# Chunk 0 of a gated network multiplied before its 1/rms is known, behind strided attention, on one core

## Chip, cores and metric

The kernel runs on one core of a Trainium2 chip. The metric is the device time of one execution in microseconds (us); several executions give a median.

## What is computed

Attention with two fixed masks on 8 batches of 8 heads, then RMS norm and a gated feed-forward network over all 4608 rows, in fp32:

```
scores = q @ k.T / sqrt(64)                # 8 x 8 heads, 576 x 576, head_dim 64
rel = pos[:, None] - pos[None, :]
mask_local   = (rel >= 0) & (rel < 32)                        # heads 0 to 3
mask_strided = (rel >= 0) & (pos[None, :] % 32 == pos[:, None] % 32)   # heads 4 to 7
attn = softmax(where(mask, scores, -1e9)) @ v
x = attn as (4608, 512)                    # batch * seq, head * head_dim
xn = x / sqrt(mean(x * x, -1) + 1e-6) * rms_g
out = (silu(xn @ w_gate) * (xn @ w_val)) @ w_out              # 512 -> 1536 -> 512
```

The weights arrive as float64.

## The kernel before

**Layout.** The 4608 rows are nine chunks of 512. x is held with the 512 model features on the partitions, as four tiles (kc = 0 to 3) per chunk. The network's 1536 inner features are twelve groups of 128, u = 0 to 11: for each u the gate product and the value product (`gemm1`, banks g and v) each take 12 multiplications of 128x512 (4 tiles times 3), then `slot_g` and `slot_h` form silu(gate) * value, and `slot_o` multiplies that with w_out into the banks a0 to a3. Each fp32 operand is split into a high and a low part (`split`), and a product is high*high + low*high + high*low, hence the 3. Chunks 0 to 2 run in this way, with weights that are read from float64 and split in chunk 0 (`convert_weights`: two ScalarE operations, then sign, merge, cast and low part); chunks 3 to 8 run two at a time with a scheme of seven products.

**Attention.** A unit is a pair of heads of one batch: `unit_s` multiplies the scores (72 small multiplications, and for units 0 to 3 two more that put the mask, `cb`, into the bank through the identity `identb`), takes maxima, exps, sums and scaled weights, and transposes on VectorE; `unit_o` multiplies with the values (80 small multiplications) and copies the result into x. Chunk 0 needs units 0 to 3. Unit 0 uses the bank pair, units 1 to 3 use a0/a1, a2/a3 and g/v; all units alternate between two buffers for exps (`pp`), two for the transpose (`pT`) and two for maxima and sums (`st`).

**Chunk 0's norm.** `square` squares each tile; its column sums go into a corner of a1 (`sums`, L663). `root0` then adds them up, takes a bit trick as a first guess of 1/sqrt and three Newton steps (L712 to L719, VectorE), spreads the result over the partitions (`spread`, L724, TensorE) and multiplies the four tiles by it and by the gain (L729). Only then `convert(0)` splits x and the first `gemm1` can start.

**Order.** Everything is issued in an order that a planner in the program (`Plan`) makes from a table of costs: it gives each operation an engine and a place in that engine's row, and the engines run their rows in order. Where TensorE would stand for long in the beginning the planner puts filling multiplications by zeros (`fill`, L470) into the row. Loads go through SyncE's queue, a few at the start through ScalarE's.

## Time and profile before

| | us |
|---|---|
| median of 3 executions | 988.3 (987.5 to 989.18) |
| the profiled execution | 984.86 |
| its span | 982.7 |

| engine | busy us | share of the span | instructions |
|---|---|---|---|
| TensorE, multiplications (PE) | 946.3 | 96% | 8621 |
| TensorE, weight loads (PEld) | 769.2 | 78% | 8621 |
| VectorE (DVE) | 726.4 | 74% | 1125 |
| ScalarE (ACT) | 450.2 | 46% | 713 |
| GpSimd (POOL) | 159.5 | 16% | 122 |

The span is what the profiler sees of the program; the execution's own time holds a little more. The chain of work that ended last is 89% TensorE and 5% VectorE. Busy shares are means over stages, so the stretches below are read one by one.

### The profile page before, as it was taken

Reading aid. Unit: us, or ns where it says so; the run is one execution under the profiler, and the core shown is the slowest. Engines: PE = TensorE matmul, PEld = TensorE weight load, DVE = VectorE, ACT = ScalarE, POOL = GpSimd, SP = SyncE. Lnnn points to the kernel's source line nnn. Section 1 sums busy time; section 2 is a strip of 40 time slices with the busy share of each in tenths; the row PEclk is TensorE's granted clock in tenths of the full one; section 3 lists DMA queues with packets and bytes.
Section 4 is the critical chain, followed back from the end, with each engine's and each line's share of the span. In section 5 each row is a group of like instructions: output and inputs, shape, how many; then the busy total and the mean of one; then the engine's idle time right before and its main releaser. Section 6 shows DMA issues by size and latency. Waiting matters only on the chain.

```text
span 982.7 us, 21097 instructions
## 1 busy us (share of the span) xinstructions
PE 946.3 (96%) x8621; PEld 769.2 (78%) x8621; DVE 726.4 (74%) x1125; ACT 450.2 (46%) x713; POOL 159.5 (16%) x122
## 2 busy tenths in 40 slices
PE   6999999999989999899999999999999999999998
PEld 5878887888768888688888777788787887888786
DVE  4599889789778997866668999545778894344783
ACT  5697665333245321644445574244444733333340
POOL 1211002023036330200003403001112020000130
PEclk8799999999989999899999999999999999999999
DMA  9746656878655848784643936974246579833631
GB/s 366 284 153 192 229 198 227 292 243 302 202 191 201 275 149 274 279 258 127 190 148 114 318 105 239 385 255 121 57 122 212 171 260 385 265 107 95 216 97 65
DMA packets 122495, 205.66 MB, mean 209 GB/s; under 512 B 10784, under 2 KB 66336, under 8 KB 119328
## 3 DMA queue, kind: packets, MB, share of 16 engines
q1 hardware_dynamic: 121680, 203.58, 62.2%
q8 instruction: 68, 1.11, 0.4%
q10 hardware_dynamic: 720, 0.74, 0.2%
q14 instruction: 27, 0.22, 0.1%
HBM read 160.24 MB, written 44.04 MB: 208 GB/s over the span
## 4 chain that ended last, share of the span: by engine, by line
PE 89%; DVE 5%; DMA 2%; ACT 2%; issue 2%; SPq 0%; ACTq 0%; DVEq 0%
PE a L1006 15%; PE g L1006 10%; PE v L1006 10%; PE v L863 9%; PE g L863 9%; PE a L900 9%; PE a L1129 8%; PE g L1129 5%; PE v L1129 4%; PE pair L605 4%; PE pair L547 3%; DVE bl L454 2%; DMA bl<-gvd 1%; PE v L470 1%; DMA to<-bl 1%
## 5 line engine op out<-in xcount | busy, mean ns | idle before, releaser
L446 ACT CAST bl<-bl 128x512 fp32r<-128x512 f32 (+1 forms) x170 | 109.6, 668 | 120.0 <-PE a L900 28.9
L1006 PE MATMUL a<-bl,bl 128*128 128x512 f32 x644 | 159.7, 393 | 0.0
L454 DVE TENSOR_TENSOR bl<-bl,bl 128x512 fp32r<-128x512 f32 x201 | 149.6, 773 | 11.8 <-ACT bl L446 3.8
L1006 PEld LDWEIGHTS a<-bl,bl 128*128 128x128 f32 x644 | 119.2, 188 | 26.1 <-ACT bl L1013 0.4
L863 PE MATMUL g<-bl,bl 128*128 128x512 f32 x432 | 114.7, 400 | 6.9 <-DVE bl L454 6.2
L1006 PE MATMUL g<-bl,bl 128*128 128x512 f32 x425 | 110.4, 394 | 6.9 <-DMA bl<-gvd 3.4
L1006 PE MATMUL v<-bl,bl 128*128 128x512 f32 x420 | 109.2, 395 | 3.8 <-DVE bl L1043 3.2
L863 PE MATMUL v<-bl,bl 128*128 128x512 f32 x432 | 112.6, 396 | 0.0
L900 PE MATMUL a<-bl,bl 128*128 128x512 f32 x432 | 109.0, 393 | 0.0
L863 PEld LDWEIGHTS g<-bl,bl 128*128 128x128 f32 x432 | 80.3, 190 | 27.0 <-DVE bl L454 8.5
L1006 PEld LDWEIGHTS g<-bl,bl 128*128 128x128 f32 x425 | 80.2, 190 | 25.6 <-DVE bl L454 5.9
L1006 PEld LDWEIGHTS v<-bl,bl 128*128 128x128 f32 x420 | 79.4, 190 | 22.5 <-DVE bl L1043 4.4
L1017 DVE TENSOR_TENSOR a<-a,bl 128x512 f32<-128x512 f32 x72 | 49.9, 697 | 63.7 <-PE a L1006 51.4
L900 PEld LDWEIGHTS a<-bl,bl 128*128 128x128 f32 x432 | 82.0, 190 | 17.9 <-DVE bl L454 0.7
L863 PEld LDWEIGHTS v<-bl,bl 128*128 128x128 f32 x432 | 80.8, 190 | 17.8 <-DVE bl L883 0.4
L963 DVE TENSOR_TENSOR bl<-bl,bl 128x512 f32<-128x512 f32 x98 | 69.4, 723 | 30.1 <-ACT bl L1022 29.7
L1129 PE MATMUL a<-bl,bl 128*128 128x512 f32 x298 | 70.3, 390 | 0.0
L454 POOL TENSOR_TENSOR bl<-bl,bl 128x512 fp32r<-128x512 f32 x23 | 33.8, 1471 | 213.6 <-PE a L1006 101.6
L448 DVE CAST bl<-bl 128x512 fp32r<-128x512 f32 (+1 forms) x90 | 48.2, 537 | 27.3 <-PE a L900 7.2
L1129 PEld LDWEIGHTS a<-bl,bl 128*128 128x128 f32 x298 | 55.9, 188 | 11.7
L963 POOL TENSOR_TENSOR bl<-bl,bl 128x512 f32<-128x512 f32 x21 | 38.8, 1847 | 116.7 <-DVE bl L963 46.5
L815 POOL TENSOR_TENSOR bl<-bl 128x256 f32<-128x256 f32 (+1 forms) x32 | 32.7, 1030 | 135.7 <-DVE bl L808 59.8
(150 smaller groups left out, 1299.6 us busy)
## 6 DMA issues: line engine op xcount, KB each, us to landing
bl<-gvd SPq DMA_DIRECT2D x252, 256.0 KB, 4.9
gvd<-bl SPq DMA_DIRECT2D x72, 256.0 KB, 4.2
bl<-to SPq DMA_DIRECT2D x72, 256.0 KB, 4.8
bl<-wos SPq DMA_DIRECT2D x54, 256.0 KB, 3.8
bl<-in_wgv_dram SPq DMA_DIRECT2D x12, 1024.0 KB, 8.6
bl<-wos SPq DMA_DIRECT2D x12, 1024.0 KB, 6.6
vt<-in_vl_dram SPq DMA_DIRECT2D x28, 320.0 KB, 3.5
xx<-in_kT_dram SPq DMA_DIRECT2D x28, 288.0 KB, 4.4
```

What stands on the lines that cost most here:

```text
L446: nc.scalar.copy(out=o, in_=i)
L448: nc.vector.tensor_copy(out=o, in_=i)
L454: elementwise(CH, lambda e: both(e).tensor_tensor(out=lo.new(F32R), in0=src(), in1=hi.f32(), op=ALU.subtract), reads + [hi.key], [lo.key])
L547: nc.tensor.matmul(out=pr[at // CH][c:c + 32, at % CH:at % CH + KW], lhsT=tq()[r, q0:q0 + 32], rhs=tk_()[r, q0:q0 + KW], start=not quick, ...
L605: nc.tensor.matmul(out=pr[s][64 * h:64 * h + 64, 32 * lo:32 * hi], lhsT=va()[r:r + 32, kb], rhs=pT[r:r + 32, 64 * kb - 32 * (kb > 0):min(6 ...
L815: elementwise(256 if ds != ALL else CH, lambda e: both(e).tensor_tensor(out=d.t[:, ds], in0=x.t[:, xs], in1=y.t[:, ys], op=ALU.subtract), ...
L863: nc.tensor.matmul(out=out_, lhsT=w.t[:, sl], rhs=x.t, start=(kc == 0 and i == 0), stop=(kc == KC - 1 and i == 2))
L900: nc.tensor.matmul(out=acc[t], lhsT=x.t[:, sl], rhs=w.t, start=(u == 0 and i == 0), stop=(u == NU - 1 and i == 2))
L963: elementwise(CH, lambda e: both(e).tensor_tensor(out=o.new() if fresh else o.t, in0=a.t, in1=b.t, op=how), [a.key, b.key], [o.key])
L1006: nc.tensor.matmul(out=banks[bk], lhsT=w, rhs=xs[k][y].t, start=start and k == 0 and i == 0, stop=stop and k == 1 and i == 2, skip_group_c ...
L1017: op("DVE", dve(CH), 0, lambda: nc.vector.tensor_tensor(out=banks[bk], in0=banks[bk], in1=t.t, op=ALU.add), reads=[t.key], writes=[bk])
L1129: nc.tensor.matmul(out=banks[bks[j]], lhsT=v, rhs=xs[k][y].t, start=start and k == 0 and i == 0, stop=stop and k == KT - 1 and i == 2, ski ...
```

## The change

1. **Chunk 0 is multiplied without its norm.** `convert0` splits each tile as soon as its unit is there, with the gain folded in; 1/rms per row is applied later: as a factor to the gate product ahead of silu (a product on VectorE with a spread copy of 1/rms), and, as the value product also lacks it, as a factor per output row where the output banks are copied out.
2. **`root0`** keeps the first four operations on VectorE; the Newton steps, now four operations each, go to GpSimd; the spread copy of 1/rms is taken by ScalarE.
3. **Units 0 to 3** use the banks g/v, a0/a1, a2/a3 and pair; units 2 and 3 get exp and transpose buffers of their own out of the pool of blocks, and four `st` tiles replace two. The u = 1 products of chunk 0 use a0 and a2, and that pass calls `slot_h` ahead of `slot_o`.
4. **Loads** come in a written order (`LOADS`): q/k of unit 0, identity and gain, mask, q/k of units 1 and 2, and so on; the first weights stand ahead of the last two values.
5. **Sign of weights:** the VectorE operation that took a sign bit out of one 32-bit word and put it into another becomes a 16-bit mask from one half-word to another; ScalarE writes the exponent's bits into the neighbouring half-word.
6. Fillings are 192 columns wide instead of 224, are counted anew, and go to the bank of the operation that follows. The choice of blocks uses `MIX` = 30 instead of 40.

```diff
-MIX = 40
+MIX = 30
-FILLS = 150.0
+FILLS = 120.0
+FILLN = 192
+LOADS = ("q0", "c2", "c0", "q1", "q2", "v0", "c1", "q3", "v1", "w", "v2", "v3")
...
     def banks_of(i):
-        k = i if i < NPRO else 0
-        if k == 0:
+        if i >= NPRO or i == NPRO - 1:
             return [pair_[:, 0], pair_[:, 1]], [SK]
-        two = (("a0", "a1"), ("a2", "a3"), ("g", "v"))[k - 1]
+        two = (("g", "v"), ("a0", "a1"), ("a2", "a3"))[i]
...
+        if 1 < i < NPRO:
+            z, y = take2(), take2()
+            pbuf_, pkeys, tbuf_, tkeys = (lambda: wide(z, None, SW)), keys_of(z), (lambda: wide(y, None, SW)), keys_of(y)
...
-            for k in range(3):
-                nc.vector.tensor_tensor(out=rz, in0=rx, in1=ry, op=ALU.mult)
-                V(out=rz, in0=rz, scalar=-0.5, in1=ry, op0=ALU.mult, op1=ALU.mult)
-                V(out=rcol if k == 2 else ry, in0=rz, scalar=1.5, in1=ry, op0=ALU.add, op1=ALU.mult)
-        op("DVE", 3200, 0, root, reads=["a1s%d" % p for p in range(4)], writes=["rcol"])
+        op("DVE", 760, 0, first, reads=["a1s%d" % p for p in range(4)], writes=["rx"])
+        def newton():
+            T = nc.gpsimd.tensor_tensor
+            for k in range(3):
+                T(out=rz, in0=ry, in1=ry, op=ALU.mult)
+                T(out=rz, in0=rz, in1=rx, op=ALU.mult)
+                nc.gpsimd.tensor_scalar(out=rz, in0=rz, scalar1=-0.5, scalar2=1.5, op0=ALU.mult, op1=ALU.add)
+                T(out=rcol if k == 2 else ry, in0=rz, in1=ry, op=ALU.mult)
+        op("Pool", 2400, 0, newton, reads=["rx"], writes=["rcol"])
...
-        for kc in range(KC):
-            rt = raw[0, kc]
-            op("DVE", dve(CH) + 60, 0, lambda kc=kc, rt=rt: nc.vector.scalar_tensor_tensor(
-                out=rt.t, in0=rt.t, scalar=gt[:, kc:kc + 1], in1=acc[3], op0=ALU.mult, op1=ALU.mult),
-               reads=["a3", "gt"], writes=[rt.key])
+        r = E["root"] = take()
+        op("ACT", act(CH, True), 0, lambda: nc.scalar.copy(out=r.new(), in_=acc[3]), reads=["a3"], writes=[r.key])
...
+    def convert0(kc):
+        rt, hi, lo, k = raw[0, kc], take(True), take(True), gt[:, kc:kc + 1]
+        op("ACT", act(CH), 0, lambda: nc.scalar.activation(out=hi.new(F32R), in_=rt.t, func=AF.Copy, scale=k), reads=["gt", rt.key], writes=[hi.key])
+        op("DVE", dve(CH), 0, lambda: nc.vector.scalar_tensor_tensor(out=lo.new(F32R), in0=rt.t, scalar=k, in1=hi.f32(), op0=ALU.mult, op1=ALU.subtract),
+           reads=["gt", rt.key, hi.key], writes=[lo.key], port=True)
+        X[kc] = hi, lo
+        give(rt)
...
-        op("DVE", dve(2 * CH), 0, lambda: nc.vector.scalar_tensor_tensor(out=cell(0), in0=cell(1), scalar=0x80000000, in1=cell(0),
-                                                                         op0=ALU.bitwise_and, op1=ALU.bitwise_or), writes=wk + [("wq", 2)], port=True)
+        op("DVE", SIGN, 0, lambda: nc.vector.tensor_scalar(out=half(1), in0=half(3), scalar1=0x8000, scalar2=None, op0=ALU.bitwise_and),
+           writes=wk + [("wq", 2)], port=True)
...
-        return key[0]
+        return {"g": "a0", "v": "a2"}[key[0]] if c == 0 and key[1] == 1 else key[0]
...
+        if c == 0:
+            r = E["root"]
+            op("DVE", dve(CH), 0, lambda: nc.vector.tensor_tensor(out=e.new(), in0=bg, in1=r.t, op=ALU.mult), reads=[bk, r.key], writes=[e.key])
+            op("ACT", act(CH), 0, lambda: nc.scalar.activation(out=e.t, in_=e.t, func=AF.Silu), writes=[e.key], tab="silu")
...
-                    copy_to(e, ob.new(), acc[t])
+                    if c:
+                        copy_to(e, ob.new(), acc[t])
+                    elif e == "ACT":
+                        nc.scalar.activation(out=ob.new(), in_=acc[t], func=AF.Copy, scale=rcol[:, t:t + 1])
+                    else:
+                        nc.vector.tensor_scalar(out=ob.new(), in0=acc[t], scalar1=rcol[:, t:t + 1], scalar2=None, op0=ALU.mult)
```

**Where the rows of the engines change.** ScalarE, from the exps of the first unit on, before. `pair`, `a_`, `g` and `v` are banks, `pp` the exp buffers, `st` maxima and sums; L565 is an exp, L446 a copy of unit 0's result into x, L772 the first operation on the first weights (`bl_217`):

```order
L565 ACTIVATE pp_69,st_76<-pair,st_76 128x64 x9
L565 ACTIVATE pp_70,st_77<-a_83,st_77 128x64 x5
L565 ACTIVATE pp_70,st_77<-a_84,st_77 128x64 x4
L565 ACTIVATE pp_69,st_76<-a_85,st_76 128x64 x5
L565 ACTIVATE pp_69,st_76<-a_86,st_76 128x64 x4
L446 COPY bl_452<-pair 128x288
L565 ACTIVATE pp_70,st_77<-g,st_77 128x64 x5
L565 ACTIVATE pp_70,st_77<-v,st_77 128x64 x4
L772 ACTIVATE bl_217<-bl_217 128x1024
```

The same place now, from the third unit's exps on (L582 is an exp, L452 a copy into x, L765 a high part of x with the gain, L808 and L812 the operations on weights):

```order
L582 ACTIVATE bl_386,st_78<-a_87,st_78 128x64 x5
L582 ACTIVATE bl_386,st_78<-a_88,st_78 128x64 x4
L582 ACTIVATE bl_461,st_79<-pair,st_79 128x64 x9
L452 COPY bl_520<-a_85 128x288
L452 COPY bl_520<-a_86 128x224
L452 COPY bl_524<-a_86 128x64
L765 ACTIVATE bl_530<-bl_514,few 128x512
L765 ACTIVATE bl_586<-bl_520,few 128x512
L808 ACTIVATE bl_217<-bl_217 128x1024
```

The four runs of exps follow one another, and copies, splitting and weights come behind them.

TensorE at the end of the prologue, now. L689 are sums of squares, L564 scores of a unit of the next chunk, L476 fillings, L901 gate and value products of u = 0 (`bl_530` and `bl_602` are high and low part of the first x tile), L754 spreads 1/rms:

```order
L564 MATMUL pair<-xx_64,xx_63 32x64 x36
L689 MATMUL a_86<-few,bl_657 128x4 x4
...
L476 MATMUL a_85<-still 128x192
L901 MATMUL g<-bl_530,bl_718 128x512 x2
L901 MATMUL g<-bl_602,bl_718 128x512
L901 MATMUL v<-bl_530,bl_718 128x512 x2
L901 MATMUL v<-bl_602,bl_718 128x512
L901 MATMUL g<-bl_586,bl_718 128x512 x2
L901 MATMUL g<-bl_646,bl_718 128x512
L901 MATMUL v<-bl_586,bl_718 128x512 x2
L901 MATMUL v<-bl_646,bl_718 128x512
L754 MATMUL a_88<-ident,few 128x128 x4
```

Before, the spreading (L724) stood between 29 and 32 fillings ahead of the first product; it now stands behind the first 12 products, and 21 fillings stand ahead of them.

VectorE at the same place, now. L814, L816, L454 and L819 are sign, merge, cast and low part of weights (`bl_217` the first set, `bl_266` the second), L766 the low part of the last x tile, L737 to L740 the start of 1/rms:

```order
L814 TENSOR_SCALAR bl_217<-bl_217 128x1024
L816 SCALAR_TENSOR_TENSOR bl_217<-bl_217 128x1024
L766 SCALAR_TENSOR_TENSOR bl_661<-bl_657,few,bl_661 128x512
L454 CAST bl_718<-bl_217 128x1024
L737 TENSOR_REDUCE few<-a_86 128x4
L738 TENSOR_SCALAR few<-few 128x4
L739 TENSOR_SCALAR few<-few 128x4
L740 TENSOR_SCALAR few<-few 128x4
L819 TENSOR_TENSOR bl_718<-bl_217,bl_718 128x1024
L588 SCALAR_TENSOR_TENSOR pp_69<-pair,cb 128x576
L591 TENSOR_REDUCE st_76<-pp_69 128x9
L814 TENSOR_SCALAR bl_266<-bl_266 128x1024
```

Before, nine Newton operations (L717 to L719) and four scalings of x (L729) stood behind L715 here; both are gone from VectorE's row, and the second weight set is not begun until the low part of the first is done.

## Rows read from the trace of the kernel before

**Rows 1.** Busy time by stretch: from and to in us, length, then per engine busy us (and instructions), granted TensorE clock as a share of 2.4 GHz, busy share of the DMA engines, GB/s.

```profile
0.00:51.00 51.00, 40.79 (x858) 35.55 (x859) 26.62 (x65) 30.26 (x96) 9.29 (x18) 0.80 0.82 314
51.00:160.00 109.00, 108.06 (x1033) 87.99 (x1033) 101.50 (x125) 77.73 (x96) 11.84 (x9) 1.00 0.59 202
160.00:983.00 823.00, 797.49 (x6733) 645.68 (x6731) 598.32 (x937) 342.24 (x522) 138.40 (x97) 0.99 0.62 204
```

**Rows 2.** TensorE's waits from 60 us on, the five longest kinds: who waited for whom, us in total, times, the longest.

```profile
PE g L863 <- DVE bl L454: 5.6, 3, 2.9
PE g L1006 <- DMA bl<-gvd: 3.4, 1, 3.4
PE v L1006 <- DVE bl L1043: 3.2, 3, 1.6
PE pair L691 <- DVE bl L448: 2.4, 2, 1.8
PE g L1006 <- DVE bl L454: 1.7, 1, 1.7
```

**Rows 3.** TensorE in order of time: start, length, line, operation, out<-in, shape, count, and in brackets the idle time before it and what ended it.

```profile
7.12 0.41 PE L541 MATMUL pair<-cb,identb 128*128 128x320 bf16 x2 [0.99 <-DMA cb<-in_consts_dram]
7.46 1.21 PE L547 MATMUL pair<-bl 64*32 64x64 f32 x72
...
42.34 4.65 PE L470 MATMUL v<-still 128*128 128x224 bf16 x29
...
47.74 3.23 PE L470 MATMUL v<-still 128*128 128x224 bf16 x32
50.74 0.71 PE L863 MATMUL g<-bl,bl 128*128 128x512 f32 x2
52.04 0.50 PE L863 MATMUL g<-bl,bl 128*128 128x512 f32 x1 [0.58 <-DVE bl L454]
```

**Rows 4.** ScalarE in order of time, columns as in rows 3.

```profile
5.44 0.30 ACT L500 CAST ident<-identb 128x128 f32<-128x128 bf16 x1 [1.80 <-DMA identb<-in_consts_dram]
9.80 0.31 ACT L565 ACTIVATE pp<-pair,st 128x64 f32<-128x64 f32 x1 [4.07 <-PE a L547]
...
16.04 0.31 ACT L565 ACTIVATE pp<-a,st 128x64 f32<-128x64 f32 x1 [0.80 <-DVE st L586]
...
21.45 0.40 ACT L446 COPY bl<-pair 128x288 f32<-128x288 f32 x1 [2.63 <-PE pair L605]
...
24.36 1.17 ACT L772 ACTIVATE bl<-bl 128x1024 f32<-128x1024 f32 x1
...
36.63 0.68 ACT L446 COPY bl<-g 128x256 f32<-128x256 f32 x2 [6.88 <-PE v L605]
37.10 0.74 ACT L446 COPY bl<-v 128x256 f32<-128x256 f32 x2
37.81 0.63 ACT L659 ACTIVATE bl<-bl 128x512 f32<-128x512 f32 x1
```

**Rows 5.** VectorE in order of time, columns as in rows 3.

```profile
42.52 0.18 DVE L712 TENSOR_REDUCE a<-a 128x4 f32<-128x16 f32 x1 [3.44 <-PE a L663]
...
44.96 0.16 DVE L719 SCALAR_TENSOR_TENSOR few<-a,few 128x4 f32<-128x4 f32 x1
...
48.01 1.41 DVE L729 SCALAR_TENSOR_TENSOR bl<-bl,few,a 128x512 f32<-128x512 f32 x2 [0.21 <-issue]
```

**Rows 6.** TensorE where it restarts after idle time that no semaphore ended ("issue"), columns as in rows 3; between the first row and the second stand seven more, with 4, 1, 1, 40, 32, 5 and 9 multiplications.

```profile
13.83 0.75 PE L547 MATMUL a<-bl 64*32 64x64 f32 x35 [2.16 <-issue]
...
20.11 1.27 PE L605 MATMUL pair<-pT,bl 32*64 32x64 f32 x71 [1.28 <-issue]
...
26.71 2.33 PE L605 MATMUL a<-pT,bl 32*64 32x64 f32 x80
...
33.03 1.28 PE L663 MATMUL a<-few,bl 128*128 128x4 f32 x11 [1.24 <-issue]
```

**Rows 7.** The DMA queue that carries instructions, in the microseconds 17 to 18 and 30 to 31: packets, MB, time as a share of 16 engines.

```profile
q8 instruction: 1, 0.02, 6.0%
...
q8 instruction: 1, 0.02, 5.5%
```

**Rows 8.** The issue of the first half of the mask through ScalarE's queue, from the DMA issues of the first 20 us: out<-in, count, KB each, us from issue to landing.

```profile
cb<-in_consts_dram ACTq DMA_DIRECT2D x1, 144.0 KB, 5.4
```

**Rows 9.** GpSimd's operations by line and shape over the whole span: count, busy us, mean ns of one, idle time before.

```profile
L815 POOL TENSOR_TENSOR bl<-bl 128x256 f32<-128x256 f32 x26 | 24.0, 933 | 93.5 <-PE v L863 55.5 <-DVE bl L815 19.5 <-DVE bl L808 17.8
...
L808 POOL TENSOR_TENSOR bl<-bl 128x1024 f32<-128x1024 f32 x5 | 12.7, 2538 | 11.0 <-DVE bl L750 9.0 <-DVE bl L700 2.0
...
L463 POOL MEMSET few<- 128x7 f32 x1 | 0.1, 105 | 0.0
```

**Rows 10.** VectorE's operations by line and shape from 0 to 165 us, columns as in rows 9.

```profile
L776 DVE SCALAR_TENSOR_TENSOR bl<-bl 128x1024 uint32<-128x1024 uint32 x18 | 21.9, 1216 | 0.7 <-ACT bl L774 0.4 <-issue 0.3
...
L883 DVE TENSOR_TENSOR bl<-bl,v 128x512 f32<-128x512 f32 x12 | 8.2, 684 | 3.8 <-PE v L863 3.7
...
L448 DVE CAST bl<-bl 128x1024 fp32r<-128x1024 f32 x6 | 4.1, 690 | 0.1
```

**Rows 11.** Busy time by stretch as in rows 1, around the fillings of rows 3.

```profile
42.00:46.00 4.00, 4.00 (x24) 3.32 (x24) 2.75 (x14) 4.00 (x5) 0.00 (x0) 0.51 0.86 269
48.00:50.00 2.00, 2.00 (x23) 2.00 (x22) 1.99 (x4) 0.56 (x2) 0.00 (x0) 1.00 0.08 25
```

More of the change, by code (lines that the diff above doesn't have):

```diff
@@ L347, in op @@
                 g = gen[home[k[1]]]
-                if g.first:
-                    continue
-                if g.fresh is True:
+                if g.fresh is True and not g.first:
                     g.fresh = fn
@@ L1219, in pair_of_chunks, with due @@
             give(dst)
-    def done(i):
-        if i == 3:
-            root0()
-            convert(0)
-    for i in range(NPRO):
-        load(i)
-        load_v(i)
+    def due(z):
+        return z[1] if z[0] == "gv" else 2 * z[1] + OLAG
+    queue = sorted([("gv", u) for u in range(NU)] + [("o", k) for k in range(KT)], key=due)
+    for z in LOADS:
+        if z[0] == "q":
+            load(int(z[1]))
+        elif z[0] == "v":
+            load_v(int(z[1]))
+        elif z[0] == "c":
+            load_consts(int(z[1]))
+        else:
+            plan.boost = WB
+            convert_weights(*queue.pop(0))
+            plan.boost = 0.0
     plan.boost = BP
@@ L1246, in prepare @@
             convert_weights(*queue.pop(0))
-    queue = sorted([("gv", u) for u in range(NU)] + [("o", k) for k in range(KT)], key=due)
     prepare(AHEAD)
```

129 lines of the change are left out of this document (79 added, 50 removed).

## The prediction

> **What bounds the kernel now.** I read the busy time by stage first, then TensorE's waits, then the rows of each engine up to the first product. The profiled execution splits into three stretches [rows 1]. Up to 51 us no product of the gated network runs, although TensorE shows 40.8 us busy: that is scores, values and filling multiplications. From 51 to 160 us TensorE is busy 108.06 of 109 us, with VectorE close behind it at 101.5 and ScalarE at 77.7. Afterwards TensorE is busy 797.5 of 823 us, and its five longest kinds of wait behind 60 us sum to 16.3 us [rows 2]. So after the first 51 us only TensorE's own work counts, and what can move the end is (1) when chunk 0's first product starts, (2) whether VectorE still feeds it, (3) those later waits.
>
> The end of the first stretch [rows 3]: 29 fillings from 42.34, the spreading multiplication, 32 fillings from 47.74, two products at 50.74 and then a wait for VectorE (the first low part of x) until 52.04. Taking those two at 0.23 us each off 52.04, the products run without a hole as if begun at **51.6**.
>
> What holds them until then is one chain: scores, exps, values, squares, their sums (TensorE, until about 42.5), VectorE's root from 42.52 to 45.1, spreading, four scalings from 48.01, splitting [rows 3, 4, 5]. In ScalarE's rows the first run of exps starts at 9.80, the third at 16.04 after 0.80 us of waiting for VectorE's use of a shared buffer, and the fourth stands behind a copy, at 21.45, that waits 2.63 us for the values of unit 0; they end at 24.36, where the first weights begin [rows 4].
>
> One more thing holds TensorE. At 13.83, 20.11 and 33.03 it restarts in the middle of a run of equal multiplications, after 2.16, 1.28 and 1.24 us in which it waited for nothing that the profile names [rows 6]. From the first restart to the second it issues 127 multiplications (35+4+1+1+40+32+5+9), from the second to the third 254, that is twice 127. In the microsecond from 17 and in that from 30, shortly ahead of two of the restarts, the instruction queue moves one packet of 0.02 MB [rows 7]. I read it as the next block of the program arriving late: between two restarts lie 6.3 us, and the block behind a boundary seems to be asked for when the boundary before it is crossed. 222 multiplications stand ahead of 13.83 (30 fillings, 74 of unit 0, 74 of unit 1, 5 fillings, 39 of unit 2), so boundaries lie at 95, 222, 349, 476, 603, 730. 95 is the 63rd of unit 0's 72 score multiplications, which begin at 7.46 and take 1.2: near 8.45, and 222 could be passed 5.4 us later; 349 6.3 us after that; 603 5.0 us after 476, the 45th of the 80 values of unit 1 that begin at 26.71: near 28.0 [rows 3, 6]. All of it with the DMA engines 0.82 busy over the stretch [rows 1].
>
> [...]
>
> **The change, step by step.**
> *First scores.* The mask was third on ScalarE's queue, landed 5.4 us after issue and held the first score to 7.12; identb, which lay behind one 288 KB load as the mask now does on SyncE's queue, let ScalarE go on at 5.44 [rows 3, 4, 8]. With 30 narrower fillings (224 to 192 columns) ending near 5.7, I take 5.9: **1.2 us earlier**.
>
> *Exps.* A run takes 2.6 us (the fourth: 21.75 to 24.36). Unit 2's scores still hit boundary 222 (104 multiplications to the end of unit 0, 178 after unit 1, 4 fillings), now at 12.6; their other half takes 0.75, the maximum about 1.1. So the runs start at 8.7, 11.4, 14.5, 17.1 and end at 19.8 instead of 24.36: own banks and buffers take away both waits.
>
> *Values.* Unit 0's follow 20 fillings; 349 is the 19th of those: 12.6+6 = 18.5. Boundary 476 falls on multiplication 46 of unit 1's 80 values: 18.5+5.7 = 24.2. 603 falls on the 79th of unit 2's: 24.2+5.7 = 29.9. A run of 80 takes 1.4, so unit 1 ends at 24.9, unit 2 at 30.0, and unit 3, behind eight sums, at about 32.
>
> *From there to the first product*, on ScalarE: four copies of unit 2 (1.35) to 31.4, the high part 0.6, the low weight bits 1.1 to 33.1, two copies of unit 3 (0.7), its square (0.6) at 34.4 [rows 4]. TensorE: unit 4's scores (1.2, bank free at 33.8), the last sums (0.9) near 36.3, then 21 fillings at 0.10 to 0.16 each [rows 3]: **39.2** (38.6 to 39.9). VectorE is not later: mask, merge, last low part, cast end near 36.7, the first four root operations 0.8 behind the sums, low weights at 38.6. The chain root, spreading, scaling, 42.5 to 51.6 before, is off the path. Gain 51.6 - 39.2 = **12.4**.
>
> *Newton on GpSimd:* twelve dependent operations on 4 columns. No row shows one; a memset of 7 columns took 0.105, a product of 256 columns 0.93, 1024 columns 2.54 [rows 9]. The line through the last two leaves 0.4 at no columns, the memset 0.1. I take 0.3, so 3.6: from 37.4 to 41.0. The spreading stands behind 12 products (2.7), so TensorE comes to it at 41.9: the fillings and those products cover the chain with 0.9 to spare. At 0.1 nothing changes; at 0.93 the chain lasts 11.2, until 48.6, and everything queued behind the spreading on TensorE, first the other 12 products of u = 0, waits 6.7. Spreading itself now lies among the products: **-0.6**.
>
> *Chunk 0 with a shorter lead.* Before, two weight sets and more were converted ahead of 51; now one is. Second gate weights: VectorE's rows from 38.6 (mask 0.75, maximum 0.75, sign 0.7, exponent's sum 0.75, merge 1.2) reach 42.5, ScalarE's cast behind the root's copy 44.3, low part 46.0. TensorE comes there at 46.4 (24 products, spreading, one unit's scores). The first output products find the low part of h 0.9 late. **-1.2** for these; 0 if VectorE keeps up, -3 if not.
>
> *VectorE's total.* 128.1 us up to 160 [rows 1]. In the order's rows up to chunk 1's splitting: 18 sign operations of 1.22 become one-source masks, +12 gate products of 0.68, three 512-column subtractions, one square's sum and nine root operations fewer, one 1024-column subtraction and three casts more. The mask's own row doesn't exist; it lies between the one-source 1024-column cast, 0.69, and the two-source form, 1.22; I take 0.69, as it too has one source [rows 10]. At 0.53 saved by a mask, 0.68 for 512 columns, 0.17 for a root operation and 0.42 for a cast that is -9.5+8.2-2.0-0.7-1.5+1.2+1.3 = -3.0, or 125; about 20 of it lies before 39.2 (26.6 before 51 now, less some five operations of 1.22 that come later and the root). From 39.2 to 150, TensorE's 111 us, 105 is 95%, as 93% now: no loss beyond the 1.2. At 1.22 for a mask it is 114, and VectorE ends chunk 0 some 3 to 5 late.
>
> *Clock.* The granted clock was 0.51 (1.2 GHz) where the 29 fillings took 4.65 and full (2.4 GHz) where the 32 took 3.23, right ahead of the products [rows 3, 11]. With 21 fillings in one place the level at the first product can't be read from before: at 2.4 GHz nothing is lost, at 1.2 the first eight products take 1.8 longer. In between: **-0.8** (0 to -1.8).
>
> *The rest costs nothing:* chunk 0's 1/rms on four output copies replaces plain copies of equal width, on engines with idle time; the weights that wait for units 2 and 3's buffers are loaded near 30, land by 44, and are first needed near 64.
>
> Sum: 12.4 - 0.6 - 1.2 - 0.8 = 9.8. The later waits I leave equal (plus or minus 4: the plan behind 160 is remade too). The profiled execution, 984.86 with a span of 982.7, becomes 975.1; it lies 3.4 under the median of 988.3, so the forecast is **978.5**.
>
> **Rivals.**
> *A* (the forecast, 0.52): 974.5 to 982.
> *B* (0.17): blocks of the program come in time. Exps end at 19.8, then VectorE's two scalings, transposes and copies bring unit 3's values to 26.3, and 7.2 as above the products to 33.5: 5.7 more, 2 given back as VectorE has less lead: 974.8, range 969 to 976. Against it: three restarts on one count. [...]
> *C* (0.18): most is given back in chunk 0. Either Newton at 0.93 (-6.7) or the mask at 1.22 (-4) or both: 982 to 988. For it: twelve operations in a chain, each waiting for the one ahead; VectorE at 93%. In the worst of it the gate waits as before and the change doesn't do what it says.
> *D* (0.13, slower in most of it): the remade plan lengthens the waits at later chunk changes, where TensorE stands for VectorE's splitting, loaded weights and evacuation. They cost 16.3 now [rows 2]; from 60% more it eats the whole gain, at double the time is 988.3 - 9.8 + 16.3 = 994.8. Against it: the code of these chunks is unchanged.
>
> **How the numbers follow.** A measurement of this kernel tells about 0.2%, 2 us, from no change. A, B and two thirds of C are faster: 0.81; the rest of C and a little of D same, 0.09; slower 0.10. The range 969 to 988 takes A, B and C; D and a little of B are out.
>
> **What would show it.** Right: four runs of exps without a hole from about 8.7; restarts without a named reason 222, 349, 476 and 603 multiplications in; the first product between 38 and 41; Newton's twelve under 4.5; TensorE over 97% busy from there to chunk 1. Wrong: a first product after 45, a wait at the spreading over 2 us, a mask row over 0.9 us, or TensorE's waits behind chunk 0 over 26 us in sum.

## The result, and the profile after

The changed kernel takes 992.53 us (median of 6 runs, 991.02 to 994.86) beside 987.26 for the kernel before (6 runs, 984.13 to 989.18): a ratio of 1.0058, 95% interval 1.0038 to 1.0079. It is slower by 5.3 us, and the forecast of 978.5 is 14 us too low. Its profiled execution took 992.79, with a span of 991.0.

Four points of time tell where that came from. The first product begins at 45.70 instead of 51.6 (the prediction's reckoning for before). The value product of u = 0 in chunk 1, by which I mark the start of that chunk, begins at 173.83 instead of 163.94, the same product in chunk 2 at 293.38 instead of 289.68. In the lines below L460 (before: L454) is VectorE's low part of x for the chunk that begins, L749 the last kind of Newton's operations on GpSimd, and L927 VectorE's product of silu(gate) and value. TensorE in the changed kernel (start, length, line, operation, count, and in brackets the idle time before it):

```profile
42.48 3.52 PE L476 MATMUL a<-still 128*128 128x192 bf16 x21
45.70 1.54 PE L901 MATMUL g<-bl,bl 128*128 128x512 f32 x3
...
50.83 1.16 PE L754 MATMUL a<-ident,few 128*128 128x128 f32 x8 [1.50 <-POOL few L749]
...
169.39 1.25 PE L901 MATMUL g<-bl,bl 128*128 128x512 f32 x3 [3.21 <-DVE bl L460]
171.13 2.86 PE L901 MATMUL g<-bl,bl 128*128 128x512 f32 x7 [0.50 <-DVE bl L460]
...
293.38 3.01 PE L901 MATMUL v<-bl,bl 128*128 128x512 f32 x12 [0.58 <-DVE bl L927]
```

And before, at the changes to chunks 1 and 2:

```profile
162.75 1.20 PE L863 MATMUL g<-bl,bl 128*128 128x512 f32 x4 [1.25 <-DVE bl L454]
...
282.20 0.96 PE L863 MATMUL g<-bl,bl 128*128 128x512 f32 x3 [1.47 <-DVE bl L454]
286.08 3.80 PE L863 MATMUL g<-bl,bl 128*128 128x512 f32 x7 [2.92 <-DVE bl L454]
```

So by these two executions: 51.6 - 45.7 = 5.9 won ahead of the first product, 112.3 against 128.1 or 15.8 lost from there into chunk 1, 125.7 against 119.6 or 6.2 won from chunk 1 into chunk 2, where the waits of 1.47 and 2.92 are gone, and 4.6 lost behind (span less 289.68, or less 293.38). The sum is -8.3, the difference of the spans.

The 15.8 are the result. Busy time from the first product to chunk 1's value product, in the kernel before (columns as in [rows 1]):

```profile
51.50:163.90 112.40, 110.26 (x1040) 89.54 (x1040) 104.90 (x128) 77.23 (x95) 13.54 (x8) 1.00 0.60 203
```

And in the changed kernel, with the two later stretches of [rows 1] under it:

```profile
45.70:173.80 128.10, 116.33 (x1052) 91.42 (x1051) 118.31 (x146) 99.19 (x94) 19.05 (x19) 0.98 0.57 200
51.00:160.00 109.00, 102.44 (x936) 81.29 (x937) 99.28 (x125) 91.35 (x85) 5.65 (x4) 1.00 0.51 177
160.00:991.00 831.00, 804.65 (x6826) 652.17 (x6824) 592.54 (x924) 355.46 (x556) 129.08 (x95) 0.99 0.62 205
```

VectorE has 13.4 us more to do there and ScalarE 22.0 (7.0 and 21.0 more when counted from 0, as the stretch now begins earlier); TensorE, at 108.06 of 109 in [rows 1], is down to 102.44. TensorE was busy 1.18 of the 4.30 us from 165.0 to 169.3, around the wait of 3.21, and behind it its granted clock is 0.61 on average (169.4 to 173.8); before, it was 1.00 at that place (162.7 to 163.9). So a part of what the change of chunk loses is the clock. From 60 us on the changed kernel's five longest kinds of wait of TensorE add up to about what [rows 2] do, 17.5 against 16.3 us:

```profile
PE v L1055 <- DMA bl<-gvd: 4.3, 2, 3.3
PE v L1055 <- DVE bl L1092: 4.2, 3, 2.3
PE g L901 <- DVE bl L460: 3.7, 2, 3.2
PE g L1055 <- DMA bl<-gvd: 2.8, 2, 2.4
PE v L901 <- DVE bl L927: 2.5, 4, 1.3
```

Where ScalarE's time went, and the mask on VectorE (by line and shape in the stretch to chunk 1: count, busy us, mean ns, idle time before). First ScalarE's operation in the kernel before, then the changed kernel:

```profile
L774 ACT ACTIVATE bl<-bl,few 128x1024 uint32<-128x1024 uint8 x12 | 15.0, 1248 | 0.0
```

```profile
L812 ACT ACTIVATE bl<-bl,few 128x1024 uint16<-128x1024 uint8 x15 | 39.8, 2650 | 0.0
...
L814 DVE TENSOR_SCALAR bl<-bl 128x1024 uint16<-128x1024 uint16 x17 | 22.8, 1343 | 1.7 <-ACT bl L812 1.7
L819 DVE TENSOR_TENSOR bl<-bl,bl 128x1024 fp32r<-128x1024 f32 x17 | 22.0, 1295 | 2.0 <-ACT bl L452 2.0
...
L927 DVE TENSOR_TENSOR bl<-bl,v 128x512 f32<-128x512 f32 x11 | 7.5, 686 | 4.7 <-ACT bl L913 4.7
```

L812 is the ScalarE operation of change 5. It takes the top byte of the low word of a float64 times 1/32, which gives the three low bits of the fp32 mantissa (*The change* wrongly calls them the exponent's bits). Writing them as half-words (16 bits) lasts 2.65 us where L774's 32-bit words lasted 1.25. The mask lasts 1.34 by its record, more than the two-source operation that it replaces (1216 ns in [rows 10]). VectorE now waits 4.7 us for ScalarE's silu (L913) and 1.7 for L812 itself. With the sign step taken back (experiment 1) both are gone, and only the wait for the cast of weights (L452) stays:

```profile
L819 DVE TENSOR_TENSOR bl<-bl,bl 128x1024 fp32r<-128x1024 f32 x17 | 21.8, 1280 | 1.7 <-ACT bl L452 1.7
...
L814 DVE SCALAR_TENSOR_TENSOR bl<-bl 128x1024 uint32<-128x1024 uint32 x17 | 20.7, 1215 | 0.1
...
L927 DVE TENSOR_TENSOR bl<-bl,v 128x512 f32<-128x512 f32 x11 | 7.4, 677 | 0.0
```

### The profile page after: what moved, and what is told of

It is laid out like the page before. It is cut to its first block, busy times and chain, and to the rows that moved or that the text cites. A ratio compares the mean times of both kernels' runs of the same rounds, so it can differ in the third digit from the quotient of the medians.

```text
span 991.0 us, 21005 instructions
## 1 busy us (share of the span) xinstructions
PE 946.4 (95%) x8581; PEld 768.0 (77%) x8581; DVE 717.8 (72%) x1102; ACT 479.6 (48%) x738; POOL 146.3 (15%) x128
## 4 chain that ended last, share of the span: by engine, by line
PE 78%; DVE 11%; ACT 4%; DMA 4%; issue 2%; POOL 1%; SPq 0%; DVEq 0%; ACTq 0%
PE a L1055 15%; PE v L1055 10%; PE g L1055 10%; PE v L901 7%; PE g L901 7%; PE a L1178 7%; PE a L944 7%; PE g L1178 4%; PE pair L631 3%; PE v L1178 3%; PE pair L564 3%; DMA bl<-gvd 3%; DVE bl L460 2%; ACT bl L812 1%; DVE bl L819 1%
## 5 line engine op out<-in xcount | busy, mean ns | idle before, releaser
L452 ACT CAST bl<-bl 128x512 fp32r<-128x512 f32 (+1 forms) x173 | 111.2, 671 | 109.1 <-DVE bl L1012 20.0
L460 DVE TENSOR_TENSOR bl<-bl,bl 128x512 fp32r<-128x512 f32 x198 | 138.3, 728 | 16.5 <-ACT bl L452 9.6
L1055 PE MATMUL v<-bl,bl 128*128 128x512 f32 x432 | 113.0, 398 | 8.4 <-DMA bl<-gvd 4.3
L901 PE MATMUL g<-bl,bl 128*128 128x512 f32 x420 | 112.1, 402 | 6.3 <-DVE bl L460 3.7
L1055 PE MATMUL g<-bl,bl 128*128 128x512 f32 x427 | 110.7, 394 | 5.1 <-DMA bl<-gvd 2.8
L901 PE MATMUL v<-bl,bl 128*128 128x512 f32 x420 | 108.5, 395 | 2.5 <-DVE bl L927 2.5
L1055 PEld LDWEIGHTS g<-bl,bl 128*128 128x128 f32 x427 | 80.4, 190 | 23.6 <-DVE bl L460 5.5
L901 PEld LDWEIGHTS g<-bl,bl 128*128 128x128 f32 x420 | 78.1, 191 | 26.1 <-DVE bl L460 5.4
L901 PEld LDWEIGHTS v<-bl,bl 128*128 128x128 f32 x420 | 77.6, 188 | 20.8 <-DVE bl L927 4.2
L460 POOL TENSOR_TENSOR bl<-bl,bl 128x512 fp32r<-128x512 f32 x22 | 35.1, 1601 | 289.7 <-PE v L1055 136.8
L454 DVE CAST bl<-bl 128x512 fp32r<-128x512 f32 (+1 forms) x83 | 44.8, 542 | 12.6 <-PE a L1178 2.8
L1178 PE MATMUL g<-bl,bl 128*128 128x512 f32 x207 | 50.0, 393 | 0.1
L1178 PE MATMUL v<-bl,bl 128*128 128x512 f32 x207 | 49.1, 389 | 0.0
```

Of the source, the lines that this page charges most:

```text
L452: nc.scalar.copy(out=o, in_=i)
L454: nc.vector.tensor_copy(out=o, in_=i)
L460: elementwise(CH, lambda e: both(e).tensor_tensor(out=lo.new(F32R), in0=src(), in1=hi.f32(), op=ALU.subtract), reads + [hi.key], [lo.key])
L901: nc.tensor.matmul(out=out_, lhsT=w.t[:, sl], rhs=x.t, start=(kc == 0 and i == 0), stop=(kc == KC - 1 and i == 2))
L1055: nc.tensor.matmul(out=banks[bk], lhsT=w, rhs=xs[k][y].t, start=start and k == 0 and i == 0, stop=stop and k == 1 and i == 2, skip_group_c ...
L1178: nc.tensor.matmul(out=banks[bks[j]], lhsT=v, rhs=xs[k][y].t, start=start and k == 0 and i == 0, stop=stop and k == KT - 1 and i == 2, ski ...
```

## Experiments

All ratios are to the kernel before, run beside it on the same chip, with a 95% interval in brackets. Theory S: the sign step (change 5) was mis-sized. The rivals L and P: the rest of the change lost it, in the later chunks (L) or ahead of the first products (P).

**1. The change without its sign step.** In the changed kernel:

```diff
-nc.scalar.activation(out=half(0), ...)
-nc.vector.tensor_scalar(out=half(1), in0=half(3), scalar1=0x8000, scalar2=None, op0=ALU.bitwise_and)
+nc.scalar.activation(out=cell(0), ...)
+nc.vector.scalar_tensor_tensor(out=cell(0), in0=cell(1), scalar=0x80000000, in1=cell(0), op0=ALU.bitwise_and, op1=ALU.bitwise_or)
```

> The changed kernel with the sign of the weights taken as before: ScalarE writes 32-bit words again and VectorE uses the two-source form; every engine's row keeps its order. Theory S (the 16-bit form is what costs: in the changed kernel ScalarE's exponent operation takes 2.6 us instead of 1.24, 18 times, 24 us in chunk 0): ScalarE's busy time between 51 and 160 us falls from 91 to about 70, chunk 1 begins near 161 instead of 174, and the time falls to 978 to 986, under the kernel before. Theory L (the remade plan of the later chunks costs): chunk 0 may get shorter, but the time stays at 989 or above. Theory P (the prologue: half clock, program blocks, Newton on GpSimd): first product still at 45 to 46 and the time 988 to 992.

The median is 981.56 (9 runs), the ratio 0.9947 [0.9927, 0.9967]. That is faster than the kernel before, as S has it, though chunk 0 gets less short than was expected: ScalarE's busy time from 51 to 160 us is 76.7 instead of 70, and chunk 1's value product comes at 169.06 instead of 161.

**2. The sign step alone**, in the kernel before: the four lines of experiment 1 the other way round.

> The kernel before with the 16-bit sign alone, in an unchanged order. Theory S: ScalarE's exponent operation takes 2.6 us here too, ScalarE has some 102 us of work from 51 to 160 us and chunk 0 becomes 4 to 12 us longer: 991 to 999. Theories L and P: the time stays within 2 us of the kernel before.

The median is 993.94 (6 runs), the ratio 1.0059 [1.0043, 1.0074], and chunk 1's value product comes at 169.70 instead of 163.94. The step alone costs what the whole change does. VectorE is busy 105.17 us between the first product and chunk 1, as before (104.90), but waits there 5.1 us for ScalarE's casts and 2.4 for the half-words, where it waited 0.3 and 0.4 before.

**3. Half of the step:** ScalarE writes 32 bits as in experiment 1, VectorE keeps the 16-bit mask.

```diff
-nc.scalar.activation(out=half(0), ...)
+nc.scalar.activation(out=cell(0), ...)
```

> The changed kernel with ScalarE writing 32-bit words, and the 16-bit mask on VectorE kept. If ScalarE's 16-bit output is the whole of the sign's cost, the exponent operation takes 1.24 us, the mask stays at 1.3, and the time is within 2 us of the run with the old sign. If the mask matters (0.1 us more per operation than the two-source form, and its hold on GpSimd), it is 2 to 4 us above that run.

The median is 984.02 (6 runs), the ratio 0.9962 [0.9948, 0.9977]. By the ratios ScalarE's half is some 9.5 of the 11 us between the changed kernel and experiment 1. The rest, 1.5 by the ratios and 2.5 by the medians, would fit what the expectation gave to the mask, but lies within the two intervals and is not shown.

**4. The forms by themselves,** behind the end of the kernel before, three times each in one execution, nothing else running: one byte in eight read, 1024 results written as 32-bit words 8 bytes apart, as 16-bit 8 bytes apart, 4 bytes apart, adjacent, and as adjacent 32-bit words; then masks on VectorE.

```diff
+            for o in (w.rearrange("p (n t) -> p n t", t=2)[:, :, 0], h.rearrange("p (n t) -> p n t", t=4)[:, :, 0],
+                      h.rearrange("p (n t) -> p n t", t=2)[:, 0:1024, 0], h[:, 0:1024], w[:, 0:1024]):
+                nc.scalar.activation(out=o, in_=src, func=AF.Identity, scale=1.0 / 32, bias=low3)
...
+            for o, i in ((h4[:, :, 1], h4[:, :, 3]), (h2[:, 0:1024, 0], h2[:, 1024:2048, 0]), (h[:, 0:1024], h[:, 1024:2048]),
+                         (w2[:, :, 0], w2[:, :, 1]), (w[:, 0:1024], w[:, 1024:2048])):
+                nc.vector.tensor_scalar(out=o, in0=i, scalar1=0x8000, scalar2=None, op0=ALU.bitwise_and)
```

> The kernel before with 30 operations of 1024 elements behind its end, three of each form, to price the forms alone. ScalarE from bytes 8 bytes apart to: 32-bit words 8 bytes apart, 16-bit words 8 bytes apart, 16-bit words 4 bytes apart, adjacent 16-bit words, adjacent 32-bit words. VectorE's 16-bit mask at 8 bytes, 4 bytes and adjacent, and the same in 32 bits at 8 bytes and adjacent. If the 16-bit width of a scattered output costs: both scattered 16-bit forms take 2.6 on ScalarE and the adjacent one 1.24 or less. If the 8-byte step costs: only that form. On VectorE, if scattered 16-bit words keep the mask from the faster rate: 1.3 scattered, under 0.7 adjacent, and 0.7 in 32 bits either way.

The first repetition on each engine, in that order (VectorE: 16-bit at 8 bytes, 4 bytes, adjacent; 32-bit at 8 bytes, adjacent):

```profile
981.62 1.19 ACT L1306 ACTIVATE bl<-bl,few 128x1024 uint32<-128x1024 uint8 x1 [0.48 <-DVE bl L448]
982.84 2.56 ACT L1306 ACTIVATE bl<-bl,few 128x1024 uint16<-128x1024 uint8 x1
985.43 1.43 ACT L1306 ACTIVATE bl<-bl,few 128x1024 uint16<-128x1024 uint8 x1
986.90 1.20 ACT L1306 ACTIVATE bl<-bl,few 128x1024 uint16<-128x1024 uint8 x1
988.13 1.21 ACT L1306 ACTIVATE bl<-bl,few 128x1024 uint32<-128x1024 uint8 x1
...
1004.88 1.30 DVE L1311 TENSOR_SCALAR bl<-bl 128x1024 uint16<-128x1024 uint16 x1 [23.29 <-ACT bl L1306]
1005.97 0.81 DVE L1311 TENSOR_SCALAR bl<-bl 128x1024 uint16<-128x1024 uint16 x1
1006.82 0.43 DVE L1311 TENSOR_SCALAR bl<-bl 128x1024 uint16<-128x1024 uint16 x1
1007.28 0.70 DVE L1311 TENSOR_SCALAR bl<-bl 128x1024 uint32<-128x1024 uint32 x1
1008.01 0.69 DVE L1311 TENSOR_SCALAR bl<-bl 128x1024 uint32<-128x1024 uint32 x1
```

It is neither the type nor the step but both: 16 bits at 8 bytes cost 2.56 on ScalarE and 1.30 on VectorE; the same bits adjacent 1.20 and 0.43, 32-bit words at either step 1.2 and 0.7. (By the starts VectorE's first mask holds the engine for 1.09, about as long as the two-source form, whose records of 1.22 overlap by 0.1.)

**5. As much ScalarE time without half-words:** experiment 1 with a second pass by factor 1 behind each scaling of weights.

```diff
 nc.scalar.activation(out=h, in_=h, func=AF.Copy, scale=2.0 ** -112)
+nc.scalar.activation(out=h, in_=h, func=AF.Copy, scale=1.0)
```

> The changed kernel with the old 32-bit sign (as e1_old_sign), and behind each of chunk 0's 18 scalings of weights a second ScalarE pass over the same 1024 32-bit words with factor 1. No 16-bit operand anywhere; ScalarE gets 18 x 1.2 = 21.6 us more in chunk 0, against 24.7 by which the 16-bit form lengthened it; the order of all rows stays. Theory ScalarE's time (the 16-bit sign costs what ScalarE needs longer, whatever it writes): ScalarE over 92 busy of the 109 us from 51 to 160, VectorE waiting for ScalarE's cast, and the time 11 x 21.6/24.7 = 9.6 above e1_old_sign, which is a ratio to before of 1.002 to 1.007. Rival, half-words in memory (16-bit writes hinder the other engines, ScalarE's own length is hidden): the ratio stays within 0.3% of e1_old_sign's 0.9947.

The median is 988.12 (10 runs), the ratio 1.0016 [1.0000, 1.0031], just under the 1.002 to 1.007 that were expected, and chunk 1's value product comes at 174.08, like the changed kernel's 173.83.

```profile
46.69:174.08 127.39, 116.34 (x1052) 91.51 (x1051) 118.60 (x147) 96.76 (x108) 18.92 (x19) 0.98 0.57 201
```

So plain length of ScalarE's work, with no half-word anywhere, does most of it: 21.1 us more there (18 passes of 1.17) lengthen the run by 6.8, where 9.6 were expected in proportion to the half-words. VectorE waits 4.0 us for silu again. What the remaining part is was not tried.

**6. Newton on VectorE** (experiment 1, twelve operations moved, other rows the same).

```diff
-T = nc.gpsimd.tensor_tensor
+T = nc.vector.tensor_tensor
-nc.gpsimd.tensor_scalar(out=rz, in0=rz, scalar1=-0.5, ...)
+nc.vector.tensor_scalar(out=rz, in0=rz, scalar1=-0.5, ...)
```

> e1_old_sign with the twelve Newton operations on VectorE, behind the low part of the first weights, instead of GpSimd; all other rows the same. Theory Newton on the path: twelve at 0.2 = 2.4 us, the root ready near 48, so TensorE's wait of 2.36 at the spreading is gone, ScalarE's copy of the root comes 3 us earlier, and the time falls by 1.5 to 2.5: a ratio to before near 0.9925. Rival, VectorE is the bound of chunk 0: the 2.4 us more on VectorE come back as waits for gate and low parts before 160, and the ratio stays at 0.994 to 0.996.

The median is 980.3 (5 runs), the ratio 0.9945 [0.9927, 0.9963]. TensorE's wait for the root, 2.36 in experiment 1, is gone:

```profile
48.81 0.84 PE L901 MATMUL v<-bl,bl 128*128 128x512 f32 x3
49.49 1.05 PE L754 MATMUL a<-ident,few 128*128 128x128 f32 x8
```

The time does not fall clear of noise. VectorE is busy 119.82 of 120.38 us from the first product to chunk 1's value product (columns as in [rows 1]):

```profile
46.11:166.49 120.38, 114.82 (x1052) 92.01 (x1051) 119.82 (x154) 79.21 (x92) 14.52 (x11) 0.98 0.60 213
```

That is what the rival, VectorE as the bound of chunk 0, expected; experiment 9 tests it from the other side.

**7. Nineteen multiplications fewer at the start,** the columns the same (experiment 1 with 11 fillings of 512 instead of 30 of 192).

```diff
-    still = sbt([P, 256], "still", BF16)
+    still = sbt([P, CH], "still", BF16)
...
+    once = []
...
 def fill(n, pad):
+    if not once:
+        once.append(n)
+        for _ in range(11):
+            nc.tensor.matmul(out=pad, lhsT=still[:, 0:P], rhs=still, start=True, stop=True, skip_group_check=True)
+        return
```

> e1_old_sign with the first 30 fillings of 192 columns replaced by 11 of 512 (the same columns, 19 multiplications fewer). Theory blocks of the program: restarts without a named reason move by exactly 19 multiplications: into unit 2's scores behind 57 of 72 (15 left, instead of 34), into unit 0's values behind 18, instead of behind 19 of the 20 fillings ahead of them, and into unit 1's values behind 65 of 80 instead of 46. Rival, contention or a wait that the profile does not name but which belongs to the operations: the restarts stay behind 38 scores, 19 fillings and 46 values, or come at the same times 12.6, 19.6 and 25.9 wherever TensorE then is.

Restarts without a named reason (the third row stands 18 values into unit 0):

```profile
10.29 1.02 PE L571 MATMUL a<-bl 64*32 64x64 f32 x57
14.25 0.65 PE L571 MATMUL a<-bl 64*32 64x64 f32 x15 [2.94 <-issue]
...
20.57 0.27 PE L638 MATMUL g<-pT,bl 32*64 32x64 f32 x1 [0.41 <-issue]
...
26.62 0.46 PE L638 MATMUL a<-pT,bl 32*64 32x64 f32 x15 [3.96 <-issue]
...
32.11 0.44 PE L638 MATMUL pair<-bl,bl 32*64 32x64 f32 x10
32.85 1.27 PE L638 MATMUL pair<-bl,bl 32*64 32x64 f32 x70 [0.29 <-issue]
```

57 of 72, 18 of 80 and 65 of 80 as expected, and a fourth at 10 of unit 3's 80, which is multiplication 603 of the program: 11 fillings, 4 x 74 scores, 4 and 20 fillings, 80 and 80 values, 14 fillings, 80 values, 8 sums, 10 values. The prediction's boundaries were 222, 349, 476 and 603. The waits belong to places in the program, not to operations. The first product begins at 44.23; the one execution took 981.25.

**8. No fillings ahead of the first product** (experiment 1).

```diff
 def fill(n, pad):
+    if pad is acc[0]:
+        return
```

> e1_old_sign without the 21 fillings ahead of the first product; all other rows the same. Theory cover (fillings only occupy TensorE while the first weights' low part is made): the first product stands for VectorE's low part until about 45.5 instead of 46.4, the spreading still waits for Newton until 51.7, and the time stays within 0.2% of e1_old_sign. Theory clock (the fillings bring the clock up): without them the products from about 44 to 50 run at 1.2 GHz, 12 products cost 2 to 3 us more; as the spreading waits 2.4 anyway, what shows is a lower granted clock behind 46 and up to 2 us more. Rival: the clock rises at the same moment whatever ran, and nothing changes.

The median is 983.16 (10 runs), the ratio 0.9959 [0.9944, 0.9974], the same as experiment 1 within what can be told.

```profile
42.73 0.78 PE L903 MATMUL g<-bl,bl 128*128 128x512 f32 x1
44.87 1.22 PE L903 MATMUL g<-bl,bl 128*128 128x512 f32 x2 [1.37 <-DVE bl L821]
45.89 1.48 PE L903 MATMUL v<-bl,bl 128*128 128x512 f32 x3
...
51.02 1.16 PE L756 MATMUL a<-ident,few 128*128 128x128 f32 x8 [1.09 <-POOL few L751]
```

Three products take 1.48 (granted clock 0.50 from 45 to 50) where 0.85 stood behind fillings, and the loss disappears in the wait for the root, which is still 1.09.

**9. The sign at the forecast's prices:** experiment 1 with a one-source mask, which leaves out the three low bits that ScalarE wrote.

```diff
-nc.vector.scalar_tensor_tensor(out=cell(0), in0=cell(1), scalar=0x80000000, in1=cell(0), ...)
+nc.vector.tensor_scalar(out=cell(0), in0=cell(1), scalar1=0x80000000, scalar2=None, op0=ALU.bitwise_and)
```

> e1_old_sign whose sign operation has one 32-bit source, so that it lasts 0.70 us as in the measurement of forms, and ScalarE's stays at 1.24: the two prices that the forecast took for this step. It leaves out the three lowest bits of the weights' mantissa, which the sign now overwrites. The order of all rows stays. Theory, the sign alone was mis-sized: VectorE, which is the bound of chunk 0 in e1_old_sign and e6_newton_vector, gets 18 x 0.53 = 9.5 us back, and the time comes to what was forecast, a ratio to before of 0.989 to 0.992. Rival, the other terms were mis-sized as well (first product at 45 instead of 39, half the clock, Newton at 7.3): the gain of VectorE is small, 0.993 to 0.996 as in e1_old_sign.

The median is 980.7 (4 runs), the ratio 0.9928 [0.9904, 0.9952]; the mask measured 0.69. Busy time from the first product to chunk 1's value product, which comes at 163.03:

```profile
44.69:163.00 118.31, 114.66 (x1052) 92.38 (x1051) 108.37 (x146) 79.07 (x92) 17.96 (x19) 0.98 0.62 216
```

VectorE has 9.9 us less to do there than in the changed kernel and ScalarE 20.1 less, and chunk 1 comes 10.8 earlier. Experiment 1 differs by VectorE's work alone, 118.29 against 108.37, and these 9.9 us are worth 1.9 by the ratios, within their intervals: VectorE is now busy 92% of the stretch and TensorE 97%, so the next bound stands close behind it. The ratio lies just above the first theory's band; its interval reaches into both.

**10, 11. True costs for the planner.** Experiment 1 with 1216 instead of 700 for the sign; the changed kernel with 2630 and 1310 instead of 1290 and 700.

```diff
-op("DVE", SIGN, 0, ...)
+op("DVE", dve(2 * CH), 0, ...)
```
```diff
-op("ACT", 1290, 0, lambda: nc.scalar.activation(out=half(0), ...
+op("ACT", 2630, 0, lambda: nc.scalar.activation(out=half(0), ...
-op("DVE", SIGN, 0, ...)
+op("DVE", 1310, 0, ...)
```

> e1_old_sign with the planner's cost of the sign operation at 1216 ns, what it takes, instead of 700: the planner gives VectorE some casts and copies less in chunk 0. Theory, VectorE overloaded by a plan that counts 18 x 0.52 = 9.3 us too little: 2 to 4 us faster than e1_old_sign, a ratio to before of 0.990 to 0.993. Rival, the planner has no room or its later chunks change by chance: 0.993 to 0.999.

> The changed kernel as it is, with the two operations of the 16-bit sign at the costs that were measured (ScalarE 2630 ns instead of 1290, VectorE 1310 instead of 700): the planner can move work from ScalarE and VectorE or spread it otherwise. Theory, the plan was misled: a third to a half of the 11 us comes back, a ratio to before of 0.999 to 1.003. Rival, the work itself is too much for the 109 us in which it must be done, wherever it is put: 1.004 to 1.008 as the changed kernel.

The first takes 984.18 (10 runs), 0.9957 [0.9936, 0.9977], so nothing is gained; chunk 1 begins 6.9 earlier than in experiment 1's execution (162.13), 3.8 of it are lost behind chunk 2, and the rest is no more than the scatter of single executions. The second takes 986.62 (10 runs), 0.9987 [0.9972, 1.0003], a little better than the 0.999 to 1.003 expected. Some 0.7% of the time comes back by the planner's choices alone, with the two operations as slow as before (2.64 and 1.38), though the first product begins at 56.96. It moved work too: up to 172.5 us VectorE is busy 130.9 instead of the changed kernel's 137.8, GpSimd 36.1 instead of 26.1. As the true cost gained nothing in the first of the two, how much of the 0.7% is the luck of one plan stays open.

**12. Experiments 6 and 7 together.**

> e7_fewer_fillings (old 32-bit sign, 11 wide fillings) with Newton on VectorE as in e6_newton_vector: the candidate for the best version. Theory, gains of the prologue carry through: first product near 44.2, no wait at the spreading near 47, 2 us more than e6_newton_vector: a ratio to before of 0.991 to 0.9935. Rival, VectorE bounds chunk 0 and gives it back as in e6_newton_vector: 0.994 to 0.996.

The median is 981.37 (9 runs), the ratio 0.9951 [0.9928, 0.9973], as in experiment 1, though the products begin at 44.03 and the root is no longer waited for. What stays is the wait at the change to chunk 1:

```profile
156.47 0.73 PE L908 MATMUL g<-bl,bl 128*128 128x512 f32 x2
159.75 1.29 PE L908 MATMUL g<-bl,bl 128*128 128x512 f32 x3 [2.55 <-DVE bl L460]
```

The points of time of all these executions:

| kernel | first product | chunk 1 | chunk 2 | span |
|---|---|---|---|---|
| before | 51.6 | 163.94 | 289.68 | 982.7 |
| 2 sign alone | 51.35 | 169.70 | 297.36 | 991.3 |
| after | 45.70 | 173.83 | 293.38 | 991.0 |
| 5 extra pass | 46.69 | 174.08 | 292.99 | 985.3 |
| 11 true costs | 56.96 | 172.50 | 290.93 | 987.0 |
| 1 old sign | 46.36 | 169.06 | 287.95 | 984.1 |
| 3 half of the step | 44.28 | 165.58 | 285.73 | 979.8 |
| 6 Newton on VectorE | 46.11 | 166.49 | 285.25 | 977.8 |
| 7 fewer fillings | 44.23 | 164.78 | 283.68 | 979.5 |
| 8 no filling | 42.73 | 166.85 | 287.02 | 981.5 |
| 10 true cost, old sign | 47.59 | 162.13 | 281.17 | 981.1 |
| 12 both | 44.03 | 164.18 | 282.75 | 978.4 |
| 9 forecast's prices | 44.69 | 163.03 | 281.94 | 977.4 |

Read down the columns: from chunk 1 to chunk 2 every kernel with the new arrangement needs 118.4 to 120.2, before and experiment 2 need 125.7 and 127.7. Chunk 1 does not follow the first product from kernel to kernel: the changed kernel begins 5.9 earlier than before and reaches it 9.9 later, experiment 11 begins 11.3 later than the changed kernel and reaches it 1.3 earlier. I read it as coming when VectorE and ScalarE are done with chunk 0. Single executions of one kernel differ by some us (experiment 1's profiled one lies 4.3 above its median, that of before some 3 below), so that smaller differences in this table are not to be read.

## Why the prediction was wrong

**The step that failed** is the sign, in *VectorE's total* and in what the sum has only once. ScalarE's half, the write to half-words, was left at the old price without a word ("the low weight bits 1.1", on the way to the first product, measured 2.56 at 32.25 us): 18 operations at 2.65 instead of 1.25 are 25 us more. The mask was put at 0.69, "as it too has one source", and measured 1.34, above the bound of 1.22. Experiment 9 gives both the forecast's prices and takes 980.7, inside the 974.5 to 982 of rival A; 992.5 less that is 11.8 of the 14 us. Rival C named the mask at 1.22 and forecast 982 to 988; by experiment 3 the mask was the smaller part of it, and no rival named ScalarE's half. Of the prediction's four signs of being wrong two came, a first product after 45 and a mask over 0.9; the wait at the spreading (1.50) and the waits behind chunk 0 (17.5 in the five longest kinds from 60 us on) did not reach their marks.

How the step turns into time: ScalarE was busy 77.73 of 109 us [rows 1], but a share of 71% over a stage did not mean room. Casts and silu stand behind L812 in ScalarE's order. VectorE waits 4.7 us for silu and 1.7 for L812, neither of which it does in experiment 1, and experiment 5 shows that 21.1 us of other ScalarE work cost 6.8. Part of it may be the plan: the planner was told 1.29 and 0.70, and experiment 11 recovers some 0.7% with the measured costs.

**Right by wrong terms.** The rest of the change gains 5 to 6 us by experiment 1 (5.2 by the ratio, 6.4 by the medians 988.01 and 981.56), or about 7 with the sign at the forecast's prices (experiment 9), against 9.8 forecast, but hardly where it was forecast. That experiment 9 lands 2 us from the forecast is in good part luck. By its execution it wins 6.9 ahead of the first product where 12.4 were forecast, loses 6.0 from there to chunk 1, wins 6.8 from chunk 1 to chunk 2, which no step forecast, and loses 2.4 behind.
- *First scores:* 5.9 forecast, 6.1 measured.
- *Exps, values:* the exps began at 8.45, 11.07, 14.52 and 17.55, against 8.7, 11.4, 14.5 and 17.1. Three of the four restarts came, at the multiplications that were forecast:

```profile
12.65 1.10 PE L564 MATMUL a<-bl 64*32 64x64 f32 x34 [1.41 <-issue]
...
25.60 0.74 PE L631 MATMUL a<-pT,bl 32*64 32x32 f32 x34 [3.94 <-issue]
```

  and between them, at 19.42 (1.33 of idle time), one behind 19 fillings as said. At the fourth place, 603, nothing is lost in the changed kernel. Experiment 7 moved the three by exactly 19 multiplications, and shows 0.29 at the fourth. So three of the four places lose 1.33 to 3.94 us in the changed kernel.
- *From there to the first product:* 45.7, not 39.2, a gain of 5.9 instead of 12.4. From 33 to 46 TensorE works nearly without a hole and at a granted clock of 0.51 (0.50 from 36 on): 80 values in 2.20 instead of the 1.4 that I took, 72 scores in 2.15 instead of 1.2, 21 fillings in 3.52. Between unit 3's values and unit 4's scores stand 16 sums, which the reckoning does not name, in 3.58. The clock was priced at the products only; it should have been applied to everything ahead of them. At the forecast's prices (sums at 0.9 for eight) these five would take about 8 us instead of the 12.7 from 33.04 to 45.70, an estimate by which some 4.5 of the 6.5 us are the clock. The rest is that unit 3's values began at 33.04 instead of some 30.6: the sums ahead of them waited 1.61 for a copy on ScalarE. Why the clock was low there was not tried.
- *Newton:* 7.3 us (43.52 to 50.78) instead of 3.6, a wait of 1.50 at the spreading instead of none. It cost nothing that experiment 6 could show.
- *Shorter lead* (-1.2): the worst miss beside the sign. The earlier start buys little because VectorE has its work for chunk 0 still before it: 118.29 of the 122.7 us in experiment 1, 119.44 of 120.15 in experiment 12. In the sum, 105 of 111 us looked like 5% of room. At the change to chunk 1 TensorE then waits 2.4 to 3.2 for VectorE's L460, where before it waited 1.25. VectorE's load alone does not make this wait: it is 2.65 in experiment 9 too, with 10 us less on VectorE.
- *VectorE's total* was right but for the mask: to chunk 1's value product it was busy 132.0 before and 128.4 in experiment 9, a difference of 3.6 against 3.0 forecast. Part of that is luck: the subtractions of 512 columns took 4.9 us less instead of 2.0, and the three more casts 4.0 more instead of 1.3 (0.42 each, where the five of before measured 0.52).
- *Later waits, left equal:* not equal. Every kernel with the new arrangement needs some 6 us less from chunk 1 to chunk 2 (table); behind that they lie from 692 to 700, mostly above before's 693.0. By these executions the gain of the new arrangement lies between chunk 1 and chunk 2, and no step forecast it; which part of the arrangement does it was not tried. Rival D had the place, with the wrong sign.

Open: by medians the sign costs 5.9 in the kernel before and 11 in the changed one; chunk 1's start says 5.8 and 5 to 9 (against experiments 1, 7 and 8). Which is nearer was not settled.
